# A recurrent-attention and ReGLU kernel on one Trainium2 core: a partition holds two neighbouring tokens in every load, and a work unit becomes 256 tokens of one sequence

## The chip, the core and the metric

The kernel runs on one core of a Trainium2 chip. Its compute engines are TensorE (PE, with its weight loads listed as PEld), VectorE (DVE), ScalarE (ACT) and GpSimd (POOL). SyncE (SP) issues most of the DMAs, and POOL issues those that load the feed-forward weights. The metric is device microseconds (us) of one execution, lower is better. Matrix operands are bf16, sums are fp32 in eight PSUM banks of 128 partitions by 512 fp32 numbers.

## What is computed

There are 4 sequences (batch), 8 heads, 768 tokens and 48 numbers a head. A gated outer-product recurrence gives 384 numbers for each of 3072 tokens, and a ReGLU feed-forward network follows:

```
f = sigmoid(f_logit)
for t in range(768):
    state = f[t][:, None] * state + outer(k[t], v[t])      # 48 x 48 for each sequence and head
    x[t]  = q[t] @ state
out = (relu(x @ w_gate) * (x @ w_val)) @ w_out               # 384 -> 1536 -> 384
```

The kernel does the recurrence in chunks of 128 tokens. Within a chunk the running sum of log(1 + exp(-f_logit)) gives the decay; k is multiplied by exp of that sum and q by exp of its negative (these products are the "hats"). Then the scores are k-hat times q-hat, masked so that a token sees only earlier tokens; the output is masked scores times v, plus q-hat times the state from the chunk before; and the new state is the old one plus k-hat times v, times the decay of the whole chunk.

## The kernel before

**Units.** A window is one chunk of 128 tokens of one sequence: 24 windows, 6 chunks (c) by 4 sequences (b). The four windows of one chunk are one group of 512 tokens for the feed-forward network; it has 6 groups.

**Two layouts.** Chunks 0 and 1 are handled by `attention_duo` (L551), two sequences at a time. `load_duo` (L444) puts two neighbouring tokens on each partition, sequence 2pr on partitions 0 to 63 and sequence 2pr+1 on 64 to 127; it is two DMAs of 64 partitions each, in pieces of 96 fp32 (384 bytes). Even and odd tokens are separate operands, so that the running sum takes four matmuls (L567, L568), the scores 32 matmuls of half height (L618), and the score part of the output 64 small ones (L646). Chunks 2 to 5 are handled one window at a time by `attention_front` (L696) and `attention` (L764). `load` (L460) puts one token of each of two sequences on a partition, in pieces of 48 fp32 (192 bytes). The running sum is then one matmul (L715) and four column sums (L718), the scores are 8 matmuls (L780).

**A window's steps.** ACT takes exp and log of f (L560, L561; L706, L708); PE makes the running sum; ACT makes the two exponentials (L573, L575; L725, L727). The hats are k or q (fp32) times the exponential (fp32), written as bf16 of 128 partitions by 384: on POOL for most windows (L737, L740), on DVE for five of the first eight passes (L579, L583). v is copied by POOL into `vpad` (L589, L772). The hats are transposed either on PE with a copy out by DVE or ACT (L598, L605 in chunks 0 and 1; L751, L756 in chunk 2) or by a transposing DMA that SP issues (L759, chunks 3 to 5). DVE multiplies the scores by the mask (L623, L785). The output goes either straight into the transposed form `xT` (L636 and L646; L807, then ACT at L657 and L824; chunks 0 to 2) or in natural form into `xn` and through a transposing DMA (L813, L817, L830, L832; chunks 3 to 5). The state takes matmuls (L684, L841), a DVE sum (L544) and a POOL product (L546).

**Feed-forward.** `ffn_hidden` (L853) does for one of 12 slices of 128 hidden columns three matmuls with w_gate, three with w_val (L865), the relu on ACT (L871) and the product on DVE into `gT` (L875). Group 0 takes slices 0 to 3 and group 1 slices 0 to 5 in halves of 256 tokens. `ffn_out` (L880) is 12 matmuls a window with w_out (L888), a copy by ACT (L898) and a store by SP (L902).

**Order.** `Plan` (L94) simulates the engines with given costs when the program is built: `add` gives each operation its engine, cost and priority, and `listed` takes at each step the operation that can begin first, ties going to the lower priority number. The result is a fixed order for each engine; on the chip every engine follows its list and waits on semaphores. A feed-forward matmul has 1000 added to its priority, so attention goes ahead of it. Four PSUM banks at most belong to the feed-forward network at a time. The loads follow each other on SP's queue in the order of `first` (L301), then by `load` with at most three under way. The weights come in thirds (`wsteps`, L300) from POOL's queue, each behind a named load: `wg0@q0.1` is the first third of w_gate, issued once q of the second pair of sequences has landed. PE gets filler matmuls on zeros (L945) in the gaps of the first 17 planned microseconds.

Of the kernel before, what the change touches and what calls it, by code (L numbers as in the profile page):

```python
# [43 lines left out]
class Rings:  # L44


    SHARE, CAP, LAND = 0.16, 3300, 1.0

    def __init__(self, busy):
        self.busy = busy  # L50
        self.made = []
        self.hw_free = self.sw_free = 0.0
        self.log = []
        self.pushed = 0

    def through(self, t, work):
        for a, b in self.busy:
            if b <= t:
                continue
            if t < a:  # L60
                if work <= a - t:
                    return t + work
                work -= a - t
                t = a
            if work <= (b - t) * self.SHARE:
                return t + work / self.SHARE
            work -= (b - t) * self.SHARE
            t = b
        return t + work

    def room(self, n):
        over = self.pushed + n - self.CAP
        for begin, end, first, count in self.log:
# [6 lines left out]
    def hw(self, at, work, n):  # L80
        begin = max(at, self.hw_free)
        self.hw_free = self.through(begin, work)
        self.log.append((begin, self.hw_free, self.pushed, n))
        self.pushed += n
        return self.hw_free + self.LAND

    def sw(self, at, work):
        begin = max(at, self.sw_free)
        self.sw_free = begin + work / 0.9
        self.made.append((begin, self.sw_free))  # L90
        return self.sw_free + self.LAND


class Plan:  # L94
# [15 lines left out]
    def link(self):  # L110
        writers, readers = {}, {}
        for op in self.ops:
# [3 lines left out]
            for d in op.follows:  # L116
                deps[d] = "order"
# [24 lines left out]
    def schedule(self, banks):  # L142
        self.link()
        for op in self.ops:
            op.deps0 = op.deps
        busy = []
        for _ in range(4):
            rings = Rings(busy)
            order = self.listed(banks, rings)
            busy = rings.made  # L150
        return order

    def listed(self, banks, rings):
# [26 lines left out]
        while left:  # L180
# [27 lines left out]
            if op.flow is not None and op.ring == "hw":  # L208
                took = max(took, rings.room(op.descs) - at)
                op.end = rings.hw(at + op.lat, op.flow, op.descs)  # L210
            elif op.flow is not None:
                op.end = rings.sw(at + op.occ + op.lat, op.flow)
            else:
                op.end = at + op.occ + op.lat
# [70 lines left out]
def bass_hgrn2_outer__then__ffn_reglu_kernel(  # L285
# [13 lines left out]
    flight = 3  # L299
# [5 lines left out]
    NC = S // C  # L305
    HD = H * D
# [4 lines left out]
    GT = B * C  # L311
    assert S % C == 0 and HD == DM == 384 and H == 8 and D == 48 and GT == 512

    VSTEP, SSTEP = 112, 96
    VW, SW = NP * VSTEP, NP * SSTEP

    sb = nc.alloc_sbuf_tensor
    NL = {"f": 4, "k": 5, "q": 5, "v": 5}
    ld = {n: sb(f"{n}_in", [128, NL[n], 2, H, D], F32) for n in "fkqv"}
    NB = 4  # L320
    bneg = sb("bneg", [128, NB, 2, H, 64], BF16)
    NE = 4
    expo = sb("expo", [128, NE, 2, HD], F32)
    NH = 6
    hats = sb("hats", [128, NH, 2, H, 64], BF16)
    NQ = 8
    qkT = sb("qkT", [128, NQ, 2, NP, C], BF16)
    NM = 4
    ptm_all = sb("ptm", [128, NM, 2, NP, C], BF16)
    ptm = [ptm_all[:, i] for i in range(NM)]  # L330
    NV = 4
    vpad = [sb(f"vpad{i}", [128, VW], BF16) for i in range(NV)]
    st = [[sb(f"st{b}_{i}", [128, SW], BF16) for i in range(2)] for b in range(B)]
    NA = 3
    dec = [sb(f"dec{i}", [128, B, NP, 2], F32) for i in range(NA)]
# [15 lines left out]
    tri = sb("tri", [128, C], BF16)  # L351
# [3 lines left out]
    seen = [sb(f"seen{i}", [128, C], BF16) for i in range(2)]  # L355
    later = [sb(f"later{i}", [128, C], BF16) for i in range(2)]
    ident = sb("ident", [128, 128], BF16)
    ones = sb("ones", [128, 1], BF16)
# [3 lines left out]
    pl = Plan({"bc": 2, "tp": 2, "s": 4, "y": 2, "kv": 2, "f": 4})  # L362
# [15 lines left out]
    def pool_t(n):  # L378
        return dict(occ=0.14 + n * 2.1 / 1000.0, lat=0.13)

    def pool_c(n):
        return dict(occ=0.06 + n * 1.04 / 1000.0, lat=0.13)
# [4 lines left out]
    def fill(eng, name, ap, value, cols, prio, key=None):  # L387
        e = engine[eng]
        add(eng, lambda: e.memset(ap, value), [], [key or name], occ=0.06 + cols / 1250.0, prio=prio)

    def triangle(t, name, base, prio, step=-1):
# [3 lines left out]
            [name], [name], occ=0.3, prio=prio)  # L395

    for t, name, base in ((upto, "upto", 0), (below, "below", -1)):
        triangle(t, name, base, -20)
        add("DVE", lambda t=t: ve.memset(t[0:64, 64:128], 0.0), [name], [name], occ=0.1, prio=-20)
    fill("POOL", "ident", ident[:], 0.0, 128, -16)  # L400
    add("POOL", lambda: gp.affine_select(out=ident[:], in_=ident[:], compare_op=ALU.not_equal, fill=1.0,
                                         base=0, pattern=[[-1, 128]], channel_multiplier=1),
        ["ident"], ["ident"], occ=0.3, prio=-16)
    for i in range(2):
        triangle(seen[i], f"seen{i}", -i, -15, -2)
        triangle(later[i], f"later{i}", 128 - i, -15, -2)
        add("DVE", lambda i=i: ve.tensor_copy(seen[i][64:128, :], later[i][64:128, :]), [f"later{i}", f"seen{i}"], [f"seen{i}"],
            occ=0.2, prio=-15)
    fill("DVE", "halves", halves[:], 0.0, 1, -15)
    for x in range(2):  # L410
        add("DVE", lambda x=x: ve.memset(halves[64 * x:64 * x + 64, x:x + 1], 1.0), ["halves"], ["halves"], occ=0.07, prio=-15)
    fill("POOL", "ones", ones[:], 1.0, 1, -5)
    triangle(tri, "tri", 0, -5)

    fill("DVE", "zeros", zeros[:], 0.0, 256, -30)
    for i in range(NB):
        fill("DVE" if i < 2 else "POOL", f"bneg{i}", bneg[:, i], 0.0, 512, -28 if i < 2 else -3)
    for i in range(NH):
        fill("DVE" if i < 4 else "POOL", f"hats{i}", hats[:, i], 0.0, 512, -17 if i < 4 else -3)
    for i in range(NV):  # L420
        fill("POOL", f"vpad{i}", vpad[i][:], 0.0, VW // 2, -8)
    for i in range(NA):
        fill("DVE", f"dec{i}", dec[i][:], 0.0, 32, -14)
# [11 lines left out]

    srcs = {"f": f_logit, "k": k, "q": q, "v": v}

    def slot_of(n, c, pr):
        return (2 * c + pr) % NL[n]

    def in_keys(n, c, b0, b1):
        return [f"{n}{slot_of(n, c, b // 2)}_{b % 2}" for b in range(b0, b1)]

    def load_duo(n, c, pr, after=()):  # L444
        t = ld[n]
        row = NL[n] * 2 * HD
        ops = []
        for x in range(2):
            b = 2 * pr + x
            src = bass.AP(tensor=srcs[n].tensor, offset=b * H * S * D + c * C * D, ap=[[2 * D, 64], [S * D, H], [1, 2 * D]])  # L450
            dst = bass.AP(tensor=t, offset=64 * x * row + slot_of(n, c, pr) * 2 * HD, ap=[[row, 64], [2 * D, H], [1, 2 * D]])
            ops.append((dst, src))
        last = tails.get("load")
        op = add("SP", lambda: [sy.dma_start(d, s_) for d, s_ in ops], [], in_keys(n, c, 2 * pr, 2 * pr + 2), occ=1.3, lat=1.5,  # L454
                 prio=c * 100, after=after, follows=[last] if last else [])
        tails["load"] = op
        dma(op, f"{n}{slot_of(n, c, pr)}", 1.64, 2, 1024)
        return op

    def load(n, c, b0, b1, after=()):  # L460
        last = tails.get("load")
        t = ld[n]
        src = bass.AP(tensor=srcs[n].tensor, offset=b0 * H * S * D + c * C * D,
                      ap=[[D, C], [S * D, (b1 - b0) * H], [1, D]])
        dst = t[:, slot_of(n, c, b0 // 2), :, :, :].rearrange("p b h d -> p (b h) d")
        op = add("SP", lambda: sy.dma_start(dst, src), [], in_keys(n, c, b0, b1),
                 occ=0.42, lat=1.5, prio=c * 100, after=after,
                 follows=[last] if last else [])
        tails["load"] = op
        dma(op, f"{n}{slot_of(n, c, b0 // 2)}", 1.14 * (b1 - b0), 1, 1024 * (b1 - b0))  # L470
        return op

    WJ = NJ // wsteps
    wsrc = {"wg": w_gate, "wv": w_val}

    def load_w(nm, s, after):
# [4 lines left out]
        else:  # L481
# [3 lines left out]
        last = tails.get("load_w")  # L485
        op = add("POOL", lambda: gp.dma_start(dst, src), [], [f"{nm}{s}"], occ=0.8, lat=1.0, prio=0 if s == 0 else 6, after=after,
                 follows=[last] if last else [])
        tails["load_w"] = op
# [547 lines left out]
```

## Time and profile before

| | |
|---|---|
| time, median of 3 runs (lowest, highest) | 207.0 us (206.6, 207.17) |
| the profiled execution's own time | 205.7 us |
| its span in the profile | 204.0 us |
| granted TensorE clock | 1.00 |
| PE, PEld busy | 191.7 us (94%), 108.5 us (53%) |
| DVE, ACT, POOL busy | 110.6, 109.0, 81.4 us |
| loads of q, k, v, f | 32 DMAs of 192 KB (`load_duo`), 32 of 384 KB (`load`) |

The span runs from the first to the last instruction of the profiled execution. Busy time is the time in which an engine had an instruction under way; matmuls overlap one another, so a matmul's own duration (379 ns for 512 columns) is longer than the pace at which matmuls follow each other (three in 0.65 us). The chain of waits goes back from the last instruction, at each step to what released it. A line of a group names the code line, the engine, the operation, what it wrote and read with the shape, the count, the busy time and the mean of one, and then the idle time before it and what ended that.

### The profile page before, as it was taken

The page shows a single profiled execution, that of the slowest core. Times are in us where ns is not written, and L with a number is a line of the kernel's source. Part 1 is how long each engine was busy: PE and PEld are TensorE (multiplying, and loading weights), DVE is VectorE, ACT ScalarE, POOL GpSimd, SP SyncE. Part 2 cuts the span into 40 slices and gives each one's busy share as a digit, 9 for nine tenths or more (in the row PEclk, how much of TensorE's full clock was granted, in tenths as well). Part 3 has the DMA queues.
Part 4 walks back from the last instruction along what each step waited for, and adds up shares of the span by engine and source line. Part 5 has one row for each costly group of instructions (what it writes and reads, how often), then busy time and mean ns, then how long its engine had stood idle before and what let it go on. Part 6 is the DMA issues. An engine that isn't in the chain of part 4 may idle for free.

```text
span 204.0 us, 4780 instructions
## 1 busy us (share of the span) xinstructions
PE 191.7 (94%) x1951; PEld 108.5 (53%) x1951; DVE 110.6 (54%) x184; ACT 109.0 (53%) x235; POOL 81.4 (40%) x121
## 2 busy tenths in 40 slices
PE   7398899999998999999999799999999999999994
PEld 2154675466686855455555455555554555444562
DVE  7979784565086969437553654472744434432300
ACT  2644349423784677875684763766553533444311
POOL 8919603902579384957335355271080000000000
DMA  4999999993899897198998997997976111111112
GB/s 119 239 240 235 221 207 206 230 227 82 191 251 207 171 211 157 36 196 164 158 219 173 156 230 172 197 213 154 224 173 141 42 39 39 39 42 39 39 59 95
DMA packets 108069, 31.76 MB, mean 156 GB/s; under 512 B 101136, under 2 KB 108048, under 8 KB 108048
## 3 DMA queue, kind: packets, MB, share of 16 engines
q1 hardware_dynamic: 104064, 27.93, 65.1%
q0 software_dynamic: 3984, 3.54, 10.6%
q8 instruction: 15, 0.25, 0.5%
q14 instruction: 6, 0.05, 0.1%
HBM read 25.95 MB, written 4.72 MB: 150 GB/s over the span
## 4 chain that ended last, share of the span: by engine, by line
PE 79%; DMA 10%; SPq 4%; ACT 2%; DVE 2%; issue 1%; POOL 0%
PE ps L865 43%; PE ps L888 21%; DMA wv<-in_moe_w_val_dram 4%; SPq L454 4%; DMA xT<-xn 3%; DMA q_in<-in_q_dram 2%; PE ps L780 2%; DVE ptm L623 2%; PE ps L715 2%; PE ps L817 1%; PE ps L813 1%; PE ps L807 1%; PE ps L646 1%; PE ps L636 1%; PE ps L598 1%
## 5 line engine op out<-in xcount | busy, mean ns | idle before, releaser
L875 DVE TENSOR_TENSOR gT<-relu,ps 128x512 bf16<-128x512 bf16 (+1 forms) x82 | 50.4, 621 | 69.4 <-PE ps L865 52.3
L871 ACT ACTIVATE relu<-ps 128x512 bf16<-128x512 f32 (+1 forms) x82 | 44.8, 546 | 34.5 <-PE ps L865 34.0
L865 PE MATMUL ps<-xT,wg 128*128 128x512 bf16 (+1 forms) x246 | 60.3, 354 | 2.3 <-DMA xT<-xn 1.1
L865 PE MATMUL ps<-xT,wv 128*128 128x512 bf16 (+1 forms) x246 | 60.1, 353 | 0.6 <-DMA wv<-in_moe_w_val_dram 0.6
L888 PE MATMUL ps<-wo,gT 128*128 128x384 bf16 x288 | 51.1, 326 | 0.0
L888 PEld LDWEIGHTS ps<-wo,gT 128*128 128x128 bf16 x288 | 27.3, 98 | 18.9 <-issue 0.2
L865 PEld LDWEIGHTS ps<-xT,wg 128*128 128x128 bf16 x246 | 22.6, 98 | 22.1 <-DMA xT<-xn 1.3
L865 PEld LDWEIGHTS ps<-xT,wv 128*128 128x128 bf16 x246 | 22.7, 98 | 21.3 <-DMA wv<-in_moe_w_val_dram 0.8
L898 ACT ACTIVATE osb<-ps 128x384 f32<-128x384 f32 x24 | 11.8, 492 | 34.6 <-PE ps L888 34.4
L737 POOL TENSOR_TENSOR hats<-k_in,expo 128x384 bf16<-128x384 f32 x16 | 15.8, 999 | 23.3 <-DMA k_in<-in_k_dram 16.5
L785 DVE TENSOR_TENSOR ptm<-ps,tri 128x512 bf16<-128x512 f32 x32 | 20.6, 684 | 6.5 <-PE ps L780 6.5
L546 POOL TENSOR_TENSOR st<-ssum,dec 128x384 bf16<-128x384 f32 x16 | 13.1, 829 | 26.8 <-DVE ssum L544 26.8
L740 POOL TENSOR_TENSOR hats<-q_in,expo 128x384 bf16<-128x384 f32 x16 | 15.7, 996 | 1.9 <-DMA q_in<-in_q_dram 1.9
L623 DVE TENSOR_TENSOR ptm<-ps,seen 128x512 bf16<-128x512 f32 x16 | 10.0, 683 | 2.5 <-PE ps L618 2.4
L579 POOL TENSOR_TENSOR hats<-k_in,expo 128x384 bf16<-128x384 f32 x5 | 5.0, 1000 | 12.5 <-ACT expo L573 12.5
L945 PE MATMUL ps<-zeros 128*128 128x512 bf16 x34 | 9.8, 432 | 0.0
L725 ACT ACTIVATE expo<-ps 128x384 f32<-128x384 f32 x16 | 7.9, 491 | 3.4 <-PE ps L718 2.1
L544 DVE TENSOR_TENSOR ssum<-ps,st 128x384 f32<-128x384 f32 x16 | 8.5, 551 | 1.7 <-PE ps L841 1.0
L727 ACT ACTIVATE expo<-ps 128x384 f32<-128x384 f32 x16 | 7.9, 493 | 0.0
L830 ACT ACTIVATE xn<-ps 128x384 bf16<-128x384 f32 x12 | 5.9, 493 | 3.5 <-PE ps L817 3.5
L772 POOL CAST vpad<-v_in 128x384 bf16<-128x384 f32 x16 | 7.6, 503 | 0.3 <-DMA v_in<-in_v_dram 0.3
L708 ACT ACTIVATE bneg<-f_in 128x768 bf16<-128x768 f32 x8 | 6.7, 840 | 0.1
(90 smaller groups left out, 179.7 us busy)
## 6 DMA issues: line engine op xcount, KB each, us to landing
out_dram<-osb SPq DMA_DIRECT2D x24, 192.0 KB, 2.2
f_in<-in_f_logit_dram SPq DMA_DIRECT2D x8, 384.0 KB, 5.4
k_in<-in_k_dram SPq DMA_DIRECT2D x8, 384.0 KB, 4.8
q_in<-in_q_dram SPq DMA_DIRECT2D x8, 384.0 KB, 5.2
v_in<-in_v_dram SPq DMA_DIRECT2D x8, 384.0 KB, 5.3
f_in<-in_f_logit_dram SPq DMA_DIRECT2D x8, 192.0 KB, 4.9
k_in<-in_k_dram SPq DMA_DIRECT2D x8, 192.0 KB, 6.4
q_in<-in_q_dram SPq DMA_DIRECT2D x8, 192.0 KB, 6.9
```

The costliest lines, as they stand in the source:

```text
L544: add("DVE", lambda: ve.tensor_tensor(tmp[:, :], kv.ap[:, 0:HD], s_old[:, :], ALU.add), [kv, f"S{b}_{(c + 1) % 2}"], [key], prio=P + 8, ** ...
L546: add("POOL", lambda: gp.tensor_tensor(t4(s_new), t4(tmp), rate, ALU.mult), [key] + dk, [f"S{b}_{c % 2}"], prio=P + 8, **pool_t(HD))
L623: last_mask[0] = add("DVE", lambda i=i, j=j, s=sj[j]: ve.tensor_tensor(ptm_all[:, m0 + i, j, :, :], s.ap[:, :].rearrange("p (n t) -> p n t ...
L737: add("POOL", lambda: gp.tensor_tensor(hk, kin[:, b % 2, :, :], ex[:, 1, :].rearrange("p (h d) -> p h d", h=H), ALU.mult), in_keys("k", c, ...
L740: add("POOL", lambda: gp.tensor_tensor(hq, qin[:, b % 2, :, :], ex[:, 0, :].rearrange("p (h d) -> p h d", h=H), ALU.mult), in_keys("q", c, ...
L785: add("DVE", lambda j=j, s=s: ve.tensor_tensor(ptm[mi][:, j, :, :], s.ap[:, :].rearrange("p (n t) -> p n t", n=NP), mask, ALU.mult), [s, " ...
L865: mm = te.matmul(bank.ap[:, 0:n], wt[:, kt, j * 128:(j + 1) * 128], xT[xi][:, kt, n0:n1], start=(kt == 0), stop=(kt == NK - 1))
L871: add("ACT", lambda: sc.activation(relu[ri][:, 0:n], gate.ap[:, 0:n], AF.Relu), [gate], [f"relu{ri}"], prio=P, **act_t(n))
L875: add("DVE", lambda: ve.tensor_tensor(gT[gi][:, j, n0:n1], relu[ri][:, 0:n], val.ap[:, 0:n], ALU.mult), [val, f"relu{ri}"], [f"gT{gi}_{j}_ ...
L888: mm = te.matmul(o[b].ap[:, 0:DM], gT[gi][:, j, b * C:(b + 1) * C], wo[:, j, :], start=(j == 0), stop=(j == NJ - 1))
L898: add("ACT", lambda b=b, oi=oi: sc.activation(osb[oi][:, :], o[b].ap[:, 0:DM], AF.Copy), [o[b]], [f"osb{oi}"], prio=P, **act_t(DM))
L945: return te.matmul(spare[:, 0:WARM], zeros[:, 0:128], zeros[:, 0:WARM], start=True, stop=True, skip_group_check=True)
```

## The change

**Units and layout.** All chunks are now handled in one way, and the two old ways are gone. A unit is 256 tokens (two windows) of one sequence, 12 units in the order of `seq`: the first 256 tokens of each of the four sequences, then the second, then the third. Two units are a feed-forward group. A partition holds two neighbouring tokens of the same sequence, and each load is one DMA over all 128 partitions with pieces of 384 bytes. At most three loads are under way from the first one on. Even tokens of both windows are one operand (i = 0), odd ones the other (i = 1).

**Units 0 to 2** (`pe_hats`) make the hats by four passes over 128 partitions and transpose them on PE, as `attention_duo` did. **The other units** need each window's 128 tokens on 128 partitions for the transposing DMA. Their hats are made by passes over 64 partitions that read partitions 64y to 64y+63 and write 64i to 64i+63: four passes for k, and four for q except in unit 6. The table `on` puts one of the four on POOL and three on DVE. v is moved in the same manner: four passes a unit of 64 partitions, one on POOL and three on ACT (one of them on DVE in unit 5). Units 0 to 2 copy parts of v a second time (`vrest`) for their state matmuls.

**The rest.** The scores are 8 matmuls a window, with one mask (`seen`) in the token order even, odd. Windows 0 to 8 and 11 to 13 go to `xT` directly, the other twelve through `xn` and the transposing DMA. The second window of a unit needs the state after the first, so that the state of the first stands between the two outputs of a unit. The weights come in quarters. `ffn_out` takes three slices at a time in place of four, only group 0 has halves (slices 0 to 2), and the fillers end at 12 planned microseconds. The planner's model of the DMA queues and some of its costs are changed with this. The core of the diff:

```diff
-    duos = (0, 1)
-    pe_hats = {2}
-    x_way = {0: "tiled", 1: "tiled", 2: "tiled", 3: "xbar", 4: "xbar", 5: "xbar"}
-    wsteps = 3
-    first = ("f0.0 k0.0 q0.0 f0.1 k0.1 q0.1 v0.0 v0.1 wg0@q0.1 wv0 wg1@v0.1 wv1 wg2 wv2 f1.0 k1.0 q1.0 v1.0 "
-             "wo0@k1.0 wo1@q1.0 wo2 f1.1 k1.1 q1.1 v1.1").split()
+    wsteps = 4
+    first = 'f0 f1 k0 q0 v1 k1 v0 wg0@v0 wv0@q0 wg1@k1 f2 q1 wv1@q1 k2 v2 wg2@v2 wv2@q1 wg3@v2 wv3@v2 wo0@v2 wo2@f2 wo1@f2 wo3@f2 f3 q3 q2 k3 v3'.split()
+    seq = [(0, 0), (1, 0), (2, 0), (3, 0), (0, 1), (1, 1), (2, 1), (3, 1), (0, 2), (1, 2), (2, 2), (3, 2)]
+    pe_hats = {0, 1, 2}
+    pe_x = {0, 1, 2, 3, 4, 5, 6, 7, 8, 11, 12, 13}
+    q_lined = {0, 1, 2, 3, 4, 5, 7, 8, 9, 10, 11}
...
+    def load(n, u, after=()):
+        b, c = seq[u]
+        t = ld[n][u % NL]
+        src = bass.AP(tensor=srcs[n].tensor, offset=b * H * S * D + c * 2 * C * D, ap=[[2 * D, 128], [S * D, H], [1, 2 * D]])
+        dst = bass.AP(tensor=t, offset=0, ap=[[2 * HD, 128], [2 * D, H], [1, 2 * D]])
+        behind = list(after) + (sent[-3:][:1] if len(sent) >= 3 else [])
+        op = chain("load", "SP", lambda: sy.dma_start(dst, src), [], [f"{n}{u % NL}"], occ=0.65, lat=1.3, prio=u * 20 - 40, after=behind)
...
+        on = dict({'even': 'PE', 'k0': 'POOL', 'k1': 'POOL', 'q0': 'POOL', 'q1': 'POOL', 'k00': 'POOL', 'k01': 'DVE', 'k10': 'DVE', 'k11': 'DVE', 'q00': 'POOL', 'q01': 'DVE', 'q10': 'DVE', 'q11': 'DVE', 'v00': 'POOL', 'v01': 'ACT', 'v10': 'ACT', 'v11': 'ACT', 'r0': 'ACT', 'r1': 'ACT', 'tk': 'DVE', 'tq': 'DVE'})
+        on.update({0: {'k0': 'DVE', 'k1': 'DVE', 'q0': 'DVE', 'tk': 'DVE', 'tq': 'ACT', 'q1': 'DVE'}, 1: {'k0': 'DVE', 'q0': 'DVE', 'tk': 'ACT'}, 4: {'k01': 'DVE'}, 2: {'r0': 'DVE', 'r1': 'DVE', 'k1': 'POOL'}, 3: {'q10': 'DVE'}, 5: {'k01': 'DVE', 'v11': 'DVE'}}.get(u, {}))
...
+                for y in range(2):
+                    lo, e = 64 * y, on[f"{n}{y}{i}"]
+                    add(e, lambda i=i, n=n, x=x, ex=ex, e=e, y=y, lo=lo: engine[e].tensor_tensor(
+                        hats[64 * i:64 * i + 64, hi, y, x, :, 0:D], by_i[n][lo:lo + 64, i, :, :],
+                        ex[lo:lo + 64, x, :].rearrange("p (h d) -> p h d", h=H), ALU.mult),
+                        [f"{n}{li}", f"exp{n}{ei}_{i}", f"hats{hi}_{y}"], [f"h{n}{hi}_{y}_{i}"], prio=P + 2, **elem_t(e, HD))
...
+            for i in range(2):
+                op = add("SP", lambda i=i: sy.dma_start(qkT[:, qi, i, :, :, :].rearrange("p x n t -> p (x n) t"),
+                                                    hats[:, hi, i, :, :, :].rearrange("p x h d -> p (x h d)"), transpose=True),
+                         hat("k", i) + hat("q", i), [f"qkT{qi}_c{i}"], prio=P + 3, occ=1.27, lat=0.6)
...
-    warm_until = 17.0
+    warm_until = 12.0
```

More of the change, by code (lines that the diff above doesn't have):

```diff
@@ L434, in dma, with chain @@
         op.flow, op.descs, op.ring = flow, descs, ring
+    def chain(line, *args, **kw):
+        last = tails.get(line)
+        tails[line] = add(*args, follows=[last] if last else [], **kw)
+        return tails[line]
     srcs = {"f": f_logit, "k": k, "q": q, "v": v}
[L438 to L457, printed above, removed]
-        return op
@@ L460, in load @@
[L460 to L471, printed above, removed]
@@ new lines, in load_w, with begin @@
+        op = chain("load_w", "POOL", lambda: gp.dma_start(dst, src), [], [f"{nm}{s}"], occ=0.79, lat=1.3,
+                   prio=-10 if s == 0 else 30, after=after)
+        dma(op, f"{nm}{s}", 7.4 / wsteps, ring="sw")
+        return op
+    done = {}
+    def begin(items):
+        for item in items:
+            item, _, behind = item.partition("@")
+            need = [done[x] for x in behind.split("&")] if behind else []
+            done[item] = load_w(item[:2], int(item[2:]), need) if item[0] == "w" else load(item[0], int(item[1:]), need)
@@ new lines, in unit @@
+        chain("state", "PE", state, hat("k", 0) + hat("k", 1) + [f"hats{hi}_{i}" for i in range(2)] +
+              [f"v_{vi}_{i}" for vi in vis for i in range(2)] + [f"vpad{vi}" for vi in vis] + ([f"vrest{oi}_{y}" for y in range(2)] if u in pe_hats else []),
+              kv, occ=0.22 * ny if u in pe_hats else 0.18 * ny, lat=PE_L, prio=P + 6, opens=kv)
+        for y in range(2):
+            out_of(u, y, P, both, vis[y], mis[y], xi, r0 + y, first_unit and y == 0)
+            if y < ny:
+                new_state(kv[y], u, y, P)
@@ L931, in bass_hgrn2_outer__then__ffn_reglu_kernel @@
+        if g == 0:
+            for r in range(0, GC, 2):
+                ffn_out(0, [r, r + 1])
     for item in pend:
```

730 lines of the change are left out of this document (306 added, 424 removed).

## The prediction

> **What bounds the kernel now.** I read the page's busy times first, then the chain of waits in order of time, then the busy time in stretches of 5 us, then the start in the timeline. On the page:
>
> ```profile
> PE 191.7 (94%) x1951; PEld 108.5 (53%) x1951; DVE 110.6 (54%) x184; ACT 109.0 (53%) x235; POOL 81.4 (40%) x121
> PE 79%; DMA 10%; SPq 4%; ACT 2%; DVE 2%; issue 1%; POOL 0%
> ```
>
> PE is busy almost throughout, and four fifths of the chain that ends last is PE. The rest of the chain lies nearly all at the start. The chain in order of time shows where:
>
> ```profile
> 9.03 5.05 DMA q_in<-in_q_dram
> 14.08 0.30 issue
> 14.38 0.45 POOL wg L486
> 14.83 0.48 issue
> 15.31 8.79 DMA wv<-in_moe_w_val_dram
> 24.15 2.14 PE ps L865 x18
> ```
>
> The sixth load lands at 14.08; only then POOL issues the first weights, and the first product with w_val begins at 24.15. From there on PE is nearly never idle. So the time is the start, plus the PE work left after it, plus a few holes, plus the last copy and store.
>
> I count PE work by the chain's paces, not by durations. A feed-forward step (three matmuls) takes 0.65 us, a half one 0.33, four matmuls of L888 0.65: 62 full and 20 half slices and 72 such fours give 80.6 + 13.2 + 46.8 = 140.6 us. Attention, a pair of sequences in chunk 0: running sum 4 x 0.16, decay sums 0.18, transposes 2 x 0.45, scores 2 x 0.64, output 0.68, state 0.45, in all 4.1; chunk 1 adds 0.93 for the old state. A window of chunk 2 takes 0.27 + 0.50 + 0.33 + 0.50 + 0.17 = 1.8; of chunks 3 and 4 0.27 + 0.33 + 0.37 + 0.17 = 1.1; of chunk 5 0.87. The sum is 8.3 + 10.1 + 7.1 + 9.0 + 3.5 = 38.0. So PE has 178.6 us of work. By 24.15 it has done 7.5 us of it, so 16.6 us are lost there; the tail after 201.13 is 2.9; the remaining 204.0 - 178.6 - 16.6 - 2.9 = 5.9 us are holes after the start.
>
> **The change part by part.**
>
> PE work. Feed-forward keeps its columns (69 full, 6 half slices: 140.5). A unit has running sum 0.65, decay sums 0.18 and scores 2 x 0.33 (full height, in place of 2 x 0.64 in chunks 0 and 1). The output is 0.50 a window when written transposed, 0.29 of it (16 of 28 matmuls) without an old state, and 0.37 in natural form. The state is 0.45 in units 0 to 2 and 0.34 after, 0.17 in the last four. The transposes, 0.90, stay in three units, where before they were in six pairs. Units 0 to 2: 3 x 3.63 = 10.9; units 3 to 7: 2.6 + 2.7 + 2.7 + 2.8 + 2.6 = 13.4; units 8 to 11: 4 x 2.4 = 9.6. That is 33.9, so **-4.1 us**. PE is on the path, so this counts in full; what replaces the transposes (18 transposing DMAs for 12) is issued by SP at 1.31 us each.
>
> The start. What must land before the first feed-forward product is f, k, q and v of unit 0, mixed with those of unit 1, seven loads, and then a quarter of each weight in place of a third. A slice of 5 us in which nothing but `load_duo` runs (5 to 10) moves 241 GB/s, so 393 KB take 1.63 us. The trace has no load of 384-byte pieces over all partitions. The nearest rows are this 241 GB/s as the slow bound, and the fastest 2 us of the trace (56 to 58, 279 GB/s, loads and stores) as the fast one: 1.41 us. I take 1.41, since both halves of the partitions are written at once there also. [...] The first f now lands at 4.93 at the latest (ACT begins there); six more by 1.41 put v0 at 13.4. From the weights' first issue to the first product with w_val took 24.15 - 14.38 = 9.8 us; three quarters of the bytes make 7.3, so that product begins at about 20.7. By then PE has done unit 0 (3.6) and the sums and k-transposes of unit 1 (1.3), with the sums of unit 2 perhaps 5.5. Lost: 15.2 in place of 16.6, **-1.4 us**.
>
> The second half of group 0. q1 is now the ninth load and goes out beside the weights. Under weights, SP's last five `load_duo` were held back by the queue, 4.3 us each from 19.84 to 41.29:
>
> ```profile
> 19.84 3.54 SPq L454 DMA_DIRECT2D v_in<-in_v_dram  x2
> 23.43 7.53 SPq L454 DMA_DIRECT2D f_in<-in_f_logit_dram  x2
> 31.00 4.21 SPq L454 DMA_DIRECT2D k_in<-in_k_dram  x2
> ```
>
> So q1 lands at 13.4 + 1.4 + 4.3 = 19 (between 16 and 22), and its hats, transpose, copy, scores, four masks, two outputs with a state between, and copy by their rows make 7 us: 26. PE meanwhile has the half slices 0 to 2 (2.0) and 3.2 of units 1 and 2: 5.2 us of work for 5.3. With later handshakes I put **+1 us** for holes (0 to 4).
>
> DVE. It gets 51 hat passes over 64 partitions (0.55 us alone: the minimum of L579; a pass has the same 384 columns for half the rows) and loses three copies of L605/L756 and the two of L407. Between 30 and 150 us DVE is busy 67.7 of 120; with 28 more it is 96, or 80%. POOL falls, from 42 passes of 1.0 us to 25, and ACT gains 35 copies of v at 0.49 by the nearest row (L830), 17 us on 109; both have room beside PE. In plain load all of it fits. But the passes are in the list of the engine that also makes the masks (L785) and gT (L875), for which PE waits. Here the trace has a warning:
>
> ```profile
> 15.94 3.43 DVE L583 TENSOR_TENSOR hats<-q_in,expo 128x384 bf16<-128x384 f32 x1
> 16.11 1.01 POOL L579 TENSOR_TENSOR hats<-k_in,expo 128x384 bf16<-128x384 f32 x1
> 17.07 1.00 POOL L583 TENSOR_TENSOR hats<-q_in,expo 128x384 bf16<-128x384 f32 x1
> 18.01 0.95 POOL L589 CAST vpad<-v_in 128x384 bf16<-128x384 f32 x2
> ```
>
> The DVE pass took 3.43 in place of 0.55, and ended 0.4 us after POOL's string of four: POOL's ran at their usual 1.0. [...] A unit puts k00, q00, a v copy and two state products on POOL, 4.2 us, against six DVE passes. PE's cover is the four feed-forward banks, about two steps or 1.3 us, and the 1.95 us strings of L888. One blocked pass a unit, by up to 2.9 us, is then mostly covered. I take **+1 us** over the nine units, between 0 and 14 (below).
>
> Loads in mid-run go from 32 DMAs of 192-byte pieces to 32 of 384. DMA is near full there (slices of 200 to 250 GB/s), and PE lost 1.15 us to one late transposing DMA (at 114.63). That hole, the 0.36 and 0.43 at 62 to 65 and the smaller mask waits may go, but 18 transposing DMAs stand in one queue with the loads. I take **-1 us** (-3 to +3).
>
> Tail: the last window's copy and store are as before, 0.
>
> Sum: -4.1 - 1.4 + 1 + 1 - 1 = **-4.5 us**. The profiled execution took 205.7 (span 204.0 and 1.7 around it), so 201.2; the median of the runs shown lies 1.3 higher, so **202.5 us**.
>
> **The rivals.**
>
> *DVE is starved (slower).* Mechanism: in units 3 to 11, DVE's passes and POOL's start on the same exponentials, each unit's DVE list stops for POOL's string, the masks and gT behind it come late, and PE runs out of banks. It decides from the point where a stop is longer than PE's cover of 1.3 us. Price: 2.9 - 1.3 = 1.6 a unit, 14 in nine units, in place of my +1: 215. For it: the 3.43. Against: POOL's string is no longer (3.3 for its first four) and five other passes meet it only in part. Half of it gives 209. Chance 0.17, of which a part would end near no change.
>
> *Loads come too late behind the weights (no change).* `q2` is the 14th load, and unit 2 needs it. If the nine loads after v0 all run beside weights at 4.3 us each from 15 us on, the sixteenth lands at 54, against 46 before, where DMA falls to a tenth; PE has 23 us of group 0 and some 10 of attention from 20.7, so it would wait near 55 for about 5 us: 207.5. For it: PE has no other work then. Against: the bytes are the same and the slices before 46 are full, so they can't end later unless the limit of three leaves the queues empty. Chance 0.10.
>
> *The start and mid-run gain in full.* [...] Chance 0.15.
>
> *The change does not do what it says:* transposing DMAs that write slower in the new layout, or DVE passes that cost more when they write other partitions, would fall under the first rival's price.
>
> **How the numbers follow.** Forecast (199 to 205) 0.58, full gain 0.15, starved DVE 0.17, late loads 0.10. A measurement of this kernel can tell about 0.3% (0.6 us) from no change. Faster: 0.58 + 0.15 and a fifth of the other two, 0.78; within 0.3%: 0.05; slower: 0.17. The range leaves out the best and the worst tenth: 196.5 to 209.
>
> **What would show it.** Right: first product with w_val near 21, L865 continuous from about 27, PE work of attention 34 us by paces, DVE passes mostly 0.55 to 1.0 us. The start is wrong if v0 lands after 15; the DVE step is wrong if the passes' mean is over 1.2 us and PE's idle time names L785 or L875's releasers. A PE busy share under 92% between 30 and 195 us would make the prediction wrong on the slow side.

## The result, and the profile after

| | before | after |
|---|---|---|
| median of the runs (lowest, highest) | 206.8 us (205.2, 207.2) | 245.1 us (242.3, 250.5) |
| the profiled execution, its span | 205.7, 204.0 us | 244.5, 242.6 us |
| granted TensorE clock, mean | 1.00 | 0.93 |

The changed kernel is slower: 1.182 times the time before, interval 1.169 to 1.195. The forecast was 202.5 (196.5 to 209). Medians and ranges here are of all executions, while the ratios leave out those that ran more than 1.5% above the fastest of their kernel; where only one is left, no ratio is given. The page of the changed kernel, in the lines that answer to those of before, with PE, the granted clock and the DMA share in 40 slices (the DMA share sums the time of packets over 16 engines, and rows below show it above 1):

```profile
PE 195.9 (81%) x1677; PEld 104.2 (43%) x1677; DVE 138.2 (57%) x225; ACT 126.6 (52%) x262; POOL 68.8 (28%) x90
...
PE   7868995999669298969519967899999999999700
...
PEclk9989997999959979999986979999999999999985
DMA  7999999993799789996999949401162111111111
...
PE 41%; DMA 33%; DVE 10%; ACT 6%; issue 2%; SPq 1%; DVEq 0%
```

PE is busy 81% of the span, not 94%, and DMA has grown from 10 to 33% of the chain that ends last. The last three slices of the PE row are 7, 0 and 0 tenths. The windows of the end say what runs there (length; busy time of PE, PEld, DVE, ACT, POOL; granted clock; DMA share; GB/s):

```profile
225.00:230.00 5.00, 3.98 (x25) 2.17 (x23) 0.00 (x0) 1.47 (x3) 0.00 (x0) 1.00 0.13 40
230.00:235.00 5.00, 0.00 (x0) 0.00 (x0) 0.00 (x0) 0.00 (x0) 0.00 (x0) 0.92 0.13 50
235.00:240.00 5.00, 0.00 (x0) 0.00 (x0) 0.00 (x0) 0.00 (x0) 0.00 (x0) 0.50 0.13 50
```

Nothing but stores is left after 229.5, and they move 50 GB/s at a DMA share of 0.13, by an estimate 2.1 of the sixteen engines over which the share is taken (0.13 x 16). The last copy of ACT ends at 229.5 and the span at 242.6: 13.1 us, where before it was 2.4 (201.62 to 204.0). The chain in order of time shows the same transfers' neighbours in mid-run:

```profile
54.16 10.51 DMA k_in<-in_k_dram
...
117.37 9.02 DMA qkT<-hats
...
146.15 6.16 DMA qkT<-hats
```

The first store goes out at 52.85. The load of k issued 1.3 us later takes 10.5 us to land, where the median before was 4.8, and the two transposing DMAs of the chain take 9.0 and 6.2 us (median before 3.3). Stores are not the only thing that makes a load late: the k issued at 26.92, beside the weights and before any store, took 10.31, and with two stores a window 10.27. The waits (engine and what it waited for, us in total, times, longest):

```profile
ACT vpad L398 <- DMA v_in<-in_v_dram: 30.0, 9, 6.2
PEld ps L632 <- DMA qkT<-hats: 19.2, 7, 5.5
PE ps L632 <- DMA qkT<-hats: 16.4, 5, 5.1
```

What changed there is a part of the diff that the prediction had passed over. The store of a window, 128 rows of `osb` to 128 tokens in a row before, now has to put even and odd tokens back in order:

```diff
-            both = [(bass.AP(tensor=out.tensor, offset=at, ap=[[DM, C], [1, DM]]), osb[oi][:, :])]
+            dst = bass.AP(tensor=out.tensor, offset=(b * S + (2 * c + w % 2) * C) * DM, ap=[[DM, 2], [2 * DM, 64], [1, DM]])
```

Its outermost count is 2, where it was 128 (C). From 230 to 240 us such stores moved 50 GB/s at a share of 0.13; in the kernel before, the last store moved 189 GB/s at a share of 0.51 (202.5 to 203.5 us).

How PE's time was lost, by stretch: the length less the PE work in it, counted by the paces of the prediction. Before, 1.0 us is lost from 24.15 to 60, 3.9 from 60 to 130 and 2.9 at the end. After, some 5.5 are lost from 21.35 to 60, 27.3 from 60 to 130, 6.7 from 130 to 156 and 13.6 at the end. A part of this is the clock: from 60 to 95 us it was 0.85 here, and 1.00 in the kernel with two stores below. The start loses 14.6, to 16.6 before; PE's whole work is 175.0, to 179.5.

### The profile page after: what moved, and what is told of

It reads as the page before. It is cut to its first block, busy times and chain, and to the rows that moved or that the text cites. A ratio compares the mean times of both kernels' runs of the same rounds, so it can differ in the third digit from the quotient of the medians.

```text
span 242.6 us, 4276 instructions
## 1 busy us (share of the span) xinstructions
PE 195.9 (81%) x1677; PEld 104.2 (43%) x1677; DVE 138.2 (57%) x225; ACT 126.6 (52%) x262; POOL 68.8 (28%) x90
## 4 chain that ended last, share of the span: by engine, by line
PE 41%; DMA 33%; DVE 10%; ACT 6%; issue 2%; SPq 1%; DVEq 0%
PE ps L750 23%; PE ps L773 14%; DMA k_in<-in_k_dram 12%; DMA f_in<-in_f_logit_dram 10%; DMA qkT<-hats 6%; DVE hats L564 5%; DMA v_in<-in_v_dram 3%; DVE gT L760 2%; DMA q_in<-in_q_dram 2%; PE ps L632 1%; ACT relu L756 1%; DVE ptm L637 1%; ACT vpad L398 1%; ACT f_in L536 1%; ACT osb L785 1%
## 5 line engine op out<-in xcount | busy, mean ns | idle before, releaser
L760 DVE TENSOR_TENSOR gT<-relu,ps 128x512 bf16<-128x512 bf16 (+1 forms) x75 | 49.3, 664 | 51.8 <-PE ps L750 37.2
L637 DVE TENSOR_TENSOR ptm<-ps,seen 128x512 bf16<-128x512 f32 x48 | 30.1, 683 | 10.2 <-PE ps L632 10.2
L398 ACT ACTIVATE vpad<-v_in 64x384 bf16<-64x384 f32 x35 | 18.2, 520 | 30.5 <-DMA v_in<-in_v_dram 30.0
L564 DVE TENSOR_TENSOR hats<-k_in,expo 64x384 bf16<-64x384 f32 x27 | 21.5, 796 | 9.7 <-DMA k_in<-in_k_dram 4.7
L632 PE MATMUL ps<-qkT 48*128 48x128 bf16 x192 | 9.1, 244 | 19.1 <-DMA qkT<-hats 16.4
L564 DVE TENSOR_TENSOR hats<-q_in,expo 64x384 bf16<-64x384 f32 x24 | 17.4, 726 | 1.3 <-ACT expo L552 0.6
L564 POOL TENSOR_TENSOR hats<-k_in,expo 64x384 bf16<-64x384 f32 x9 | 10.7, 1192 | 21.5 <-ACT expo L550 15.1
L632 PEld LDWEIGHTS ps<-qkT 48*128 48x128 bf16 x192 | 6.6, 107 | 23.6 <-DMA qkT<-hats 19.2
L536 ACT ACTIVATE f_in<-f_in 128x768 f32<-128x768 f32 x12 | 10.1, 842 | 5.5 <-DMA f_in<-in_f_logit_dram 5.4
L399 POOL CAST vpad<-v_in 64x384 bf16<-64x384 f32 x12 | 7.0, 582 | 18.9 <-DMA v_in<-in_v_dram 18.8
L730 ACT ACTIVATE xn<-ps 128x384 bf16<-128x384 f32 x12 | 5.8, 487 | 12.2 <-DMA xT<-xn 12.2
L550 ACT ACTIVATE expo<-ps 128x384 f32<-128x384 f32 x24 | 10.6, 490 | 1.5 <-PE ps L546 1.3
L552 ACT ACTIVATE expo<-ps 128x384 f32<-128x384 f32 x24 | 10.8, 509 | 0.0
```

The source lines that it names most:

```text
L398: return sc.activation(out, src, AF.Copy)
L536: add("ACT", lambda cut=cut: sc.activation(raw["f"][:, cut], raw["f"][:, cut], AF.Exp, scale=-1.0), [f"f{li}"], [f"f{li}"], prio=P, **act_ ...
L552: add("ACT", lambda i=i, ex=ex: sc.activation(ex[:, 0, :], bc[i].ap[:, 0:HD], AF.Exp, scale=-1.0), [bc[i]], [f"expq{ei}_{i}"], prio=P + 1. ...
L564: add(e, lambda i=i, n=n, x=x, ex=ex, e=e, y=y, lo=lo: engine[e].tensor_tensor(hats[64 * i:64 * i + 64, hi, y, x, :, 0:D], by_i[n][lo:lo + ...
L632: mm = te.matmul(sj[j].ap[:, p * C:(p + 1) * C], tokens(u, y, 1, p, lo, lo + D), tokens(u, y, 0, p, lo, lo + D))
L637: add("DVE", lambda y=y, j=j, s=sj[j]: ve.tensor_tensor(ptm[mis[y]][:, j, :, :], s.ap[:, :].rearrange("p (n t) -> p n t", n=NP), seen[:].u ...
```

## The experiments

The ratios are to the kernel before, run on the same chip. "Two stores" is the changed kernel with the store mended as below; the later kernels start from it.

**The store alone.** Theory A: the store's pattern. Theory B: the prediction's rival, DVE's hat passes blocked by POOL's. One run writes each window as 128 plain rows (the order of the rows in the output is left unmended), one writes it by two DMAs of 64 rows (the output is the reference's), and one gives the kernel before the new pattern (its rows come out in another order).

```diff
-ap=[[DM, 2], [2 * DM, 64], [1, DM]]
+ap=[[DM, C], [1, DM]]                                    # s1
+two DMAs, i = 0, 1: offset + i * DM, ap=[[2 * DM, 64], [1, DM]]   # s2
```

> The changed kernel with one edit: each window's store writes its 128 rows one after the other (destination of 128 rows) in place of two interleaved sets of 64 (destination of 2 by 64 rows). The order of the instructions on every engine is the same; the rows of a window come out even tokens first, then odd. Theory A (the store's destination with two rows outermost is carried by two of the 16 DMA engines, and stores block those two for the loads behind them in the same queue): the tail after the last matmul falls from 13.6 to about 3 us, the waits for loads and transposing DMAs after 53 us fall from some 30 to under 10 us, and the time from 245 to 203-212. Theory B (DVE held up by POOL is the main loss): only the tail goes, 233-236. Theory C (the transposing DMAs in one queue with the loads): as B, 232-236.

> The changed kernel with each store issued as two DMAs of 64 rows of 1536 bytes (even tokens, odd tokens), so that the outermost count of each is 64. The result is the reference's. Theory A: as with the plain store, plus SP's issue time for 24 more DMAs of about 0.5 us, partly beside other work: 204-214. Theory B or C: 233-236.

> The kernel before with one edit: its store gets the destination of 2 by 64 interleaved rows; rows of a window come out permuted. Theory A: stores clog the queue here too; the last four stores take about 4 us each, so the tail grows from 2.9 to 13-14 us, and loads behind stores come late: 218-245. Theory B or C: the tail at most, so 207 if the store isn't to blame, or 217 if only the tail is.

Measured: plain rows 214.1 us, ratio 1.032 (1.024 to 1.039); two stores 215.1, 1.040 (1.036 to 1.045); the kernel before with the new store 259.9, 1.257 (1.251 to 1.264). So the store explains 30 to 31 of the 38 us, and by itself it costs the old kernel 53, more than was expected. That kernel has the waits of the changed one, though none of its loads, hats or units were touched (0.8 us on this row before):

```profile
PEld ps L780 <- DMA qkT<-hats: 21.2, 6, 6.8
```

With two stores the copy of the last window ends 3.2 us before the span does. Theory A holds for the larger part; both times lie 1 to 2 us above its ranges. Some 8 us against the kernel before, and 12.6 against the forecast, are left.

**Hats off POOL.** The two passes a unit that POOL made go to DVE, the store stays as it is.

```diff
-'k00': 'POOL', ... 'q00': 'POOL'
+'k00': 'DVE', ... 'q00': 'DVE'
```

> The changed kernel with the hat passes k00 and q00 moved from POOL to DVE, so that POOL keeps only the state products and one v copy of a unit; the order of the engines is planned anew. Theory A: the stores still clog, no gain beyond 5 us either way: 238-250. Theory B (POOL's hats hold DVE's up): DVE passes fall back to 0.55 us and the time to 215-230. Theory C: 238-250.

Measured 244.5 us, 1.183 (1.175 to 1.192): no change. The passes themselves did get shorter. First the changed kernel's group, then this one's (count, then busy time and mean ns of one):

```profile
L564 DVE TENSOR_TENSOR hats<-k_in,expo 64x384 bf16<-64x384 f32 x27 | 21.5, 796 | 9.7 <-DMA k_in<-in_k_dram 4.7
```

```profile
L564 DVE TENSOR_TENSOR hats<-k_in,expo 64x384 bf16<-64x384 f32 x36 | 21.5, 598 | 3.0 <-ACT expo L550 1.4 <-ACT expo L552 1.0
```

POOL does slow DVE's passes, 796 to 598 ns, but a third more of them in the same 21.5 us is no gain. So the 38 us do not come from theory B. The stores still clog in this run, so it does not show what the blocking costs of the 8 us that are left; hats off POOL with two stores was not run.

**One edit at a time on two stores.** Theory D: DVE's passes fill it (95% busy from 60 to 130 us); hats of units 3 to 11 by four passes over 128 rows in place, which leaves out the move of rows. Theory E: the hole at 37 us, where PE stands idle. And the planner's cost of a pass.

```diff
+e = "DVE" if i and u not in pe_hats else on[f"{n}{i}"]     # e1: 128 rows, not moved
+occ=0.75 for a pass on DVE, in place of 0.465               # e2
-... wo0@v2 wo2@f2 wo1@f2 wo3@f2 f3 q3 q2 k3 v3
+... f3 q3 q2 k3 v3 wo0@k3 wo2@f2 wo1@f2 wo3@f2             # e5
```

> The changed kernel with two stores a window, and in units 3 to 11 the hats made by four passes over 128 partitions in place (two on POOL, two on DVE) in place of eight over 64 that move rows: it leaves out the move, so that the hats of these units stand in the even/odd order and the values are not the reference's. Theory D (DVE is full from 60 to 130 us because of the 51 passes, 38 us of its time, and PE waits for masks and products behind them): DVE busy falls by some 25 us, PE's idle time between 60 and 130 from 11 to under 5 us, the time from 215 to 205-209. Theory E (the rest is lost at 37-45 us, where unit 3's k lands late and PE is idle and then slow): 213-216. Theory C (18 transposing DMAs): 213-216.

> Two stores a window, and the planner told 0.75 us for a hat pass on DVE (measured mean, in place of 0.465); the work is the same, only the fixed order of the engines changes. Theory D: the passes still take DVE's time, but PE's list puts feed-forward work where DVE is late: 209-214. If the planner's cost is the whole of it: 203-208. Theory E or C: 213-216.

> Two stores a window, and the four quarters of w_out issued only after k of unit 3 has landed, so that fewer bytes stand beside the loads of units 2 and 3. Theory E: k of unit 3 lands 3-5 us sooner, the hole at 37-40 and the slow clock after it go: 208-212. Theory D: the hole goes, DVE's stretch from 60 on stays: 210-213. Theory C: 213-216.

Measured: without moves 212.5 us, 1.028 (1.020 to 1.037), although DVE's work fell from 137.6 to 115.5 us; with the planner's cost 214.1, 1.037 (1.030 to 1.044); with w_out later 215.4, 1.046 (1.036 to 1.056). None of these is the cause alone. Giving POOL more of the passes (`k10` and `q10` of units 3 to 11) has no measured time, so what it is worth stays open.

**Transposes, order, holds.** Theory C: the transposing DMAs. Theory F: the fixed order puts attention too early. Theory G: SP is held by the loads' wait for the third load before.

```diff
-sy.dma_start(qkT..., hats..., transpose=True)
+sy.dma_start(qkT..., hats...)                               # f3: no transposition
-return end + self.LAND
+return end + (self.LAND if at < 25 else 2.5)                # f5
-prio=P + 1000
+prio=P                                                      # f6, three places
-(sent[-3:][:1] if len(sent) >= 3 else [])
+(sent[-3:][:1] if len(sent) >= 3 and u < 4 else [])         # f7
```

> The two-store kernel, in which the 18 transposing DMAs of the hats (units 3 to 11) are replaced by 18 plain DMAs of the same two tiles, 128 rows of 2 KB; the transposition itself is left out, so scores and outputs are other numbers. Order on every engine is the same. Theory C (the transposing DMAs, 1.3 to 6.7 us of SP's time each and 4.4 us to their landing, hold the loads behind them in SP's queue and the scores on PE): 206 to 210 us, and the loss of PE between 60 and 130 us, 14.5 us in the two-store kernel, under 8. Theory F (the fixed order on PE puts attention as early as its planned latencies allow, and any step that is later than planned leaves PE idle): 212 to 215, since only one of the late steps is mended. Theory G (the loads' own waits for the third load before): 213 to 216.

> The two-store kernel with one constant of its planner changed: from 25 us on a DMA is taken to land 2.5 us after its transfer instead of 1.0, so that the fixed order puts more FFN products ahead of whatever waits for a load or a transposing DMA. No instruction is added or removed. Theory F: 207 to 212 us. Theory C: 213 to 216, as the DMAs themselves stay as they are. Theory G: 213 to 216.

> The two-store kernel with the 1000 taken off the priority number of the FFN's products on PE, so that they compete with attention by their due times, and attention is spread over more of the run. No instruction is added or removed. Theory F: 205 to 211 us, with attention ending later than 133 us and the loss between 60 and 130 us under 9. Theory C or G: 212 to 217.

> The two-store kernel without the wait of each load of units 4 to 11 for the third load before it (the wait for its buffer stays). SP waited about 27 us in all at its loads, nearly all of it for other loads. Theory G (SP held by these waits issues the transposing DMAs and stores late): 207 to 212 us. Theory C: 213 to 217, as loads then lie thicker in front of the transposing DMAs. Theory F: 212 to 216.

Measured: plain DMAs 214.9 us, 1.037 (1.028 to 1.044), so C is not the cause by itself: eighteen transpositions less gain nothing. Late landing 214.3, 1.034 (1.027 to 1.042): at most a little. The other two cost time. FFN by due time took 224.7, 1.085 (1.077 to 1.093), about 10 us more. Loads not held took 225.3 (221.0 to 227.1): its fastest execution is 6 us above the fastest with two stores (214.6), the median 10. G falls: the hold of the loads saves time. F is not refuted by f6, since that order has losses of its own (11.0 us from 60 to 95, 9.2 after 156), but f5 gives it little support.

**Two edits together.** In the kernel without moves the waits named DMAs (ACT's v copies 11.1 us); in the one with late landing they named DVE's masks. Theory H: each hides the other. Theory I: the transfers, at a DMA share above 1, pace attention. All four of these leave the moves out.

```diff
+no moves, and LAND 2.5 (c1) or 4.0 (c2)
+c1 with warm_until = 17.0 in place of 12.0                  # c3
+c1 with w_out sent as in e5                                 # c4
```

> The kernel without row moves and the late landing put together (two stores a window). In the kernel without row moves DVE has 115.5 us of work instead of 137.6, and what is left of PE's and ACT's waits names DMAs (ACT's v copies 11.1 us, PE's scores 14.6 us); in the one with late landing these are gone, and what is left names DVE (its masks 18 us). Theory H (two separate late steps, each of which fills the room that the other leaves: passes on DVE, and DMAs planned too early): the two together gain more than their sum of 3.4 us against 215.1, so 206 to 210 us, and the loss between 60 and 130 us under 8 (12.2 and 11.2 each alone). Theory I (DMA transfers at a share of 1.0 and more between 20 and 120 us set the pace of attention, whatever the order): 211 to 214.

> As the run before, with a landing taken 4.0 us after the transfer instead of 2.5, which is about what the profiles show for loads (4.1 to 4.7 us from issue to landing). Theory H: within 1.5 us of the run before. Theory I: 211 to 215.

> The kernel without row moves and with late landing, and PE's filler products go on to 17 us as in the kernel before, instead of 12. Theory J (the granted clock, 0.91 over the first 20 us here and 1.00 before, comes from PE's pauses between 12 and 20 us): clock 0.97 or more over the first 20 us and 0.5 to 1.5 us less than the run without it. Otherwise the two are the same within 0.5 us.

> The kernel without row moves and with late landing, and the four w_out quarters sent after unit 3's k instead of ahead of units 2 and 3's last loads. With the two stores alone this gained nothing (215.4 for 215.1), as the hole came back at 80 us. Theory H: 1 to 3 us less than without it, since what filled the room there is mended here. Theory I: no difference.

Measured: c1 210.5 us, 1.026 (1.019 to 1.034); c2 211.9 (208.1 to 212.4); c3 212.6, 1.033 (1.021 to 1.045); c4 213.3, 1.036 (1.024 to 1.048). c1 is the sum of its parts within the intervals, 4.5 us to 3.4, where H had asked for more than the sum. The fillers of c3 brought the clock of the first 20 us from 0.91 to 1.00, and the time did not fall: theory J had the clock right and the price wrong. Between H and I this is still open.

**Half of the loads.** The loads of units 4 to 11 bring 4 of 8 heads, in the two-store kernel (i1) and in c1 (i2); in the kernel before the loads of its last three chunks are halved (i3). Instructions and order on PE, DVE, ACT and POOL stay.

```diff
-ap=[[2 * D, 128], [S * D, H], [1, 2 * D]]
+ap=[[2 * D, 128], [S * D, H if u < 4 else H // 2], [1, 2 * D]]
```

> The two-store kernel, in which each load of units 4 to 11 brings only the first 4 of 8 heads; the other heads' values are left as an earlier unit left them, so outputs are other numbers. Every instruction on PE, DVE, ACT and POOL and their order is the same. Theory I (the transfers, at a DMA share of 1.0 to 1.2 from 20 to 120 us, set the pace of attention, so the order's FFN products run out or wait behind late steps): 205 to 209 us, the loss between 60 and 130 us under 8 (14.5 now), and attention's end before 125 us. Theory H (DVE's passes and masks are late by themselves, DVE being busy 95% of that stretch): 212 to 215.

> The kernel without row moves and with late landing (210.5 us), with the loads of units 4 to 11 cut to 4 of 8 heads in the same way; it leaves out the row moves and half of these loads. Theory I: 203 to 206 us, and the loss between 60 and 130 us (14.7) under 6. Theory H alone: 209 to 211.

> The kernel before, with the loads of chunks 3 to 5 cut to 8 of their 16 pairs of batch and head (half of the data left out); all else the same. Here PE loses about 4 us between 60 and 130 us at a DMA share of 0.7 to 1.0, so both theories expect 203 to 207 us; a larger gain would say that half loads speed anything up and that the runs beside it tell nothing of the change.

Measured: i1 214.9 us, 1.042 (1.037 to 1.047), no change against 215.1. i2 **203.5 us**, 0.986 (0.983 to 0.990), 7 us less than c1. i3 206.3, 0.999 (0.995 to 1.003), so that half loads alone speed nothing up. The windows from 60 to 130 us show why i1 gained nothing. Before, then two stores, then i1, c1 and i2 (columns as above):

```profile
60.00:95.00 35.00, 33.92 (x496) 20.50 (x489) 24.59 (x45) 24.34 (x63) 24.68 (x32) 1.00 0.87 171
95.00:130.00 35.00, 33.85 (x281) 18.51 (x279) 18.09 (x29) 21.19 (x46) 14.96 (x20) 1.00 0.92 177
```

```profile
60.00:95.00 35.00, 31.06 (x349) 15.38 (x352) 33.22 (x51) 27.75 (x61) 17.84 (x19) 1.00 1.05 243
95.00:130.00 35.00, 28.76 (x297) 15.87 (x300) 33.84 (x53) 24.63 (x53) 12.42 (x14) 1.00 0.98 204
```

```profile
60.00:95.00 35.00, 31.38 (x358) 15.51 (x355) 32.70 (x50) 27.91 (x59) 16.47 (x18) 1.00 0.73 154
95.00:130.00 35.00, 29.07 (x291) 15.58 (x289) 33.34 (x52) 26.68 (x59) 14.63 (x16) 1.00 0.66 146
```

```profile
60.00:95.00 35.00, 28.77 (x332) 14.86 (x336) 26.36 (x40) 25.49 (x58) 15.41 (x18) 1.00 1.11 223
95.00:130.00 35.00, 29.91 (x306) 17.14 (x310) 24.08 (x37) 25.18 (x54) 12.53 (x14) 1.00 1.00 220
```

```profile
60.00:95.00 35.00, 33.50 (x396) 17.77 (x395) 31.24 (x47) 30.64 (x66) 16.96 (x19) 1.00 0.85 173
95.00:130.00 35.00, 34.87 (x342) 19.61 (x340) 25.90 (x39) 26.19 (x58) 12.69 (x14) 1.00 0.65 135
```

Read the DVE column (the third busy time) against the DMA share (the last but one number). With two stores both are high: 33 of 35 us, and 1.05. (A share of 1.05 is no limit by itself, since the same kernel has 1.25 from 30 to 40 us.) Half loads bring DMA to 0.7 and leave DVE at 33: PE gains nothing. No moves and late landing bring DVE to 24 to 26 and leave DMA at 1.0 to 1.1: PE gains nothing in these windows either. Only with both does PE run through, 33.5 and 34.9 of 35 us. By paces, i2 loses 2.9 us there and i1 12.5; the kernel before loses 3.9. (Of two stores and c1, some 20 matmul records are missing, so that their losses, 14.5 and 14.7, are read nearly 2 us too high. Counted by the weight loads, of which none is missing, both lose 12.8, i1 12.6 and i2 3.2.)

So neither H nor I holds alone: I had 205 to 209 for i1, H had 209 to 211 for i2, and both missed. Half of the loads gains nothing beside the moves and the early order (215.1 to 214.9) and 7 us without them (210.5 to 203.5): two limits lie over one another, and taking one away gains little. What it is in the loads that holds the kernel, and which of c1's two edits counts once they are halved, was not separated. And i2 leaves out part of the computation, so it isn't a version to use: none of the kernels here that compute the reference's output beat the kernel before.

## Why the prediction was wrong

**The step that failed is the last: "Tail: the last window's copy and store are as before, 0."** The store was not as before. It cost 30 us: about 10.7 of it in the tail, where the stores had piled up, and the rest in mid-run (PE loses 27.3 us from 60 to 130, with two stores 12.8; from 130 to 156 it loses 6.7 and 1.6). That the store's pattern is the cause is shown by the three runs; how it delays the loads is not shown. The DMA engines were busy for less than half of the time while a load was under way: from 56 to 60 us, with the k of 54.16 still to land, the DMA share was 0.47 at 133 GB/s. An estimate from the share of 0.13 and the page: of its 33.3 MB, 4.7 are stores, 2.4 MB on each of two engines; the other 28.6, if they are spread evenly over sixteen, are 1.8 MB on each. The prediction counted every instruction of attention, but looked at a DMA's bytes and pieces and not at the shape of the store's pattern. The rival of "transposing DMAs that write slower in the new layout" was the right kind of mishap at the wrong DMA, and it had no price of its own.

**Start, -1.4: right in sum.** The first product with w_val begins at 21.35 (20.7 was forecast, 24.15 before). SP's issues at the start, and that product in the timeline of PE:

```profile
4.40 0.37 SPq L460 DMA_DIRECT2D q_in<-in_q_dram  x1
5.61 0.37 SPq L460 DMA_DIRECT2D v_in<-in_v_dram  x1
6.82 0.41 SPq L460 DMA_DIRECT2D k_in<-in_k_dram  x1
```

```profile
21.35 0.50 PE L750 MATMUL ps<-xT,wv 128*128 128x256 bf16 x3 [0.45 <-DMA wv<-in_moe_w_val_dram]
```

Each load is issued when the third before it has landed, so 1.21 us is the pace of a load here: faster than both bounds, 1.41 and 1.63. That writing both halves of the partitions at once is what counts was the author's argument, and no run separates it. No row of the trace before prices the full gain (chance 0.15, and in part the low end of the range, 196.5); the loads came at 1.21 each and the start gained 2.0 us in sum. One of the six steps took 1.89, and v0 had landed by 12.67, when the first weights go out (13.4 was forecast). The weights then took longer, 8.7 us from there to that product in place of 7.3. The two misses partly cancel, which is luck. The start lost 14.6 us instead of 16.6.

**PE work, -4.1: right.** By paces it is 175.0 against 179.5.

**The hole behind q1, +1: mis-sized and misplaced.** q1 had landed by 15.73, not 19. The hole came at 37 us, where PE had 0.52 us of work in 3.0. The chain shows how it came about:

```profile
26.92 10.31 DMA k_in<-in_k_dram
...
37.25 0.55 DVE hats L564
37.81 0.60 DVE qkT L399
...
39.85 1.04 PE ps L632 x16
40.89 3.16 PE ps L750 x9
...
46.09 1.94 PE ps L750 x9
```

Unit 3's k, issued at 26.92 beside the weights, landed at 37.2. DVE's fixed list has the first hat pass of unit 3 ahead of the copies (L399) of unit 2's transposes, which PE had ended at 36.1. So DVE stood for k, and PE stood 2.48 us for those copies. From 21.35 to 40 us 4.0 us are lost, to 0.5 before from 24.15 to 40: about +3.5, inside the stated 0 to 4. It is nearer to the rival of late loads than to this step.

**DVE, +1: wrong in its reason.** The 3.43 us row before was read as POOL blocking DVE. The prediction's own sign of that, passes with a mean over 1.2 us, did not come: they took 0.80 and 0.73. What counts is load: the step said that "in plain load all of it fits", at 80% from 30 to 150 us, but it priced a pass at 0.55 us, and passes took 0.72 to 0.78 beside POOL with two stores; and attention is done at 136 us there instead of 160, so that the work lies in a shorter stretch, at 95% from 60 to 130 us.

**Loads in mid-run, -1: wrong in sign.** Larger pieces did not make room. Attention ran ahead into a stretch where the transfers (share 1.02) and DVE (95%) are both high, and 76 us of feed-forward products alone are left for the end (43 before); that PE lacked these in its pauses is our reading, and no run shows it. PE's loss from 60 to 130 us, 12.8 to 3.9, is as large as the other 8 us; how it divides between this step and DVE's is not shown. With both limits taken away, and part of the work with them, i2 took 203.5 us, close to a forecast that had counted about nothing for either.

## What to carry to other kernels

When a layout changes, look at the pattern of every DMA that touches it, the stores at the end too: an outermost count of 2 cost 30 of the 38 us here, and two DMAs of 64 rows mend it. A single edit that gains nothing does not show that what it removes is free, if a second limit lies behind it: take both away before either is dismissed, and run the same cut in the old kernel as the control.

## What the runs showed of the hardware

From 230 to 240 us stores whose outermost count was 2 moved 50 GB/s at a share of 0.13; with two stores a window, the DMAs of 64 rows landed 2.2 us after their issue (median). Passes over 64 partitions that write to other partitions cost as much as those over 128: 0.55 us at the shortest for both on DVE; on ACT the v copies take 0.52, where a copy over 128 partitions (L730) takes 0.49. And at PE's pause of 2.48 us the granted clock was 0.95, in the 5 us behind it 0.69, and then 1.00 (the columns as above):

```profile
37.00:40.00 3.00, 0.52 (x6) 0.15 (x6) 2.70 (x5) 0.60 (x1) 2.63 (x2) 0.95 1.25 204
40.00:45.00 5.00, 5.00 (x44) 2.13 (x40) 4.94 (x9) 2.02 (x4) 1.33 (x2) 0.69 1.24 210
45.00:50.00 5.00, 5.00 (x60) 2.84 (x60) 2.84 (x6) 3.68 (x7) 0.83 (x1) 1.00 1.16 206
```

The windows hold different work, so the chain above is the fair comparison: nine equal feed-forward matmuls took 3.16 us from 40.89 and 1.94 from 46.09. So this place cost 2.5 us of standing and about 1.2 in slower matmuls; that the pause brought the clock down is a reading. In i2 PE stood for only 1.5 us at this point, and the clock was 1.00 from 20 to 60 us.
